# Layer 1's recombination: two 128x256 VectorE instructions out of PSUM become one 128x512 sum, and GpSimd makes the rank-1 term

## The chip, the cores and the metric

The kernel runs on one core of a Trainium2 chip. The metric is the time of one execution on the device, in microseconds (us); a run gives the median of several executions.

Five engines work side by side, each through its own fixed row of instructions: TensorE (PE in the profile, with its weight loads as PEld), VectorE (DVE), ScalarE (ACT), GpSimd (POOL) and SyncE (SP), which issues the DMA transfers. They meet through semaphores. An instruction that waits holds up everything behind it on its engine.

## The reference, cut to what matters

A two-dimensional FFT of `x` (2 x 3008 x 256, the real part is kept) gives 6016 tokens of 256 numbers. Two dense layers follow:

```python
h = x @ w_in;   g = np.maximum(h, 0) ** 2;            x1 = g @ w_out        # layer 1, d_ff = 2048
h = x1 @ w_in2; P = a0 + a1*h + a2*h**2 + a3*h**3
Q = 1 + |b0|*|h| + |b1|*h**2;  out = (P / (Q + 1e-6)) @ w_out2              # layer 2, d_ff = 2048
```

## The kernel before, in words

**Number format.** Every matrix product is made of fp32r passes: an operand is split into a high and a low part (`hi`, `lo`), and three of the four cross products are added up in PSUM.

**Tiling.** The tokens lie along the free dimension: tile 0 has 384 columns, tiles 1 to 11 have 512. `d_ff` is cut into 16 blocks of 128, so layer 1 has 16 groups per tile, written (t, j). Layer 2 works on half tiles of 256 columns and takes two blocks of `d_ff` at a time, 8 groups per half tile, with operands of 128x512 again.

**Layer 1, tiles 3 to 11.** Mirrored frequencies are used: a tile of 512 columns holds 256 columns and their 256 mirror images. The PE makes only two half products of 128x256 in one bank of PSUM (line 771): p, from the part that is even under mirroring, and b, from the odd part. The first 256 columns of h are p + b. The other 256 are p + x0*beta - b, where x0*beta is a rank-1 term (a row of tokens, held on all partitions in `X0[t]`, times a column of weights `beta[:, i]`). Tiles 0 to 2 (`DIRECT`) make both halves on the PE and skip this recombination. In each of the 9 x 16 = 144 groups of tiles 3 to 11:

- `e1_b` (ACT, L805) copies b out of PSUM into `bc` (3 buffers);
- `e1_s`, part 0 (DVE, L814) adds p out of PSUM and b into the left half of `g` (2 buffers);
- `e1_s`, part 1 (DVE, L817) makes x0*beta + p out of PSUM into the right half. It is the last reader of the PSUM bank, so it frees it;
- `e1_s`, part 2 (POOL, L820) subtracts b from the right half;
- `e1_relu` (ACT, L829), then two squares: `e1_gh` (ACT, L835, the high part of g) and `e1_g` (ACT, L839, the full g);
- `e1_lo` (POOL, L844; DVE for tiles 0 and 1) makes the low part;
- six PE matmuls of 512 columns (L796 into o1a, o1b) add the group to the tile's output.

**Layer 2.** The PE makes h (L741), and then about a dozen elementwise instructions of 128x512 follow, six of them on DVE: t2 (L881), t3 (L885), q (L873), gh (L907), m (L913) and e (L920). gh reads two operands out of SBUF; the others take h out of its PSUM bank as one operand, which e frees. c2 (POOL, L924) makes the low part, and the PE adds the group to the output (L796 into o2a). In the last two half tiles gh moves to POOL (L905) and two rows change form (L918, L898). ACT makes the copies, absolute values, reciprocal roots and squares (L862, L867, L877, L890, L894).

**Banks.** From tile 3 on, h of layer 1, h of layer 2 and the FFT pieces take turns in five PSUM banks (p0 to p3 and o2b). A row on the PE that needs a bank waits for whoever reads it last.

**Order.** All instructions belong to named operations with an engine, needs and buffers; `ORDER` is a table that fixes each engine's row of operations. The program is issued from it, and the engines then run freely under semaphores. Layer 2 of tile t needs the whole layer 1 of tile t, so layer 2 runs about one tile behind. Behind the last tile's layer 1 stand two half tiles of layer 2 that have only themselves.

**Start.** In the first 150 us the FFT's first stage, the unpacking of both layers' weights (DVE and ACT) and the direct tiles overlap.

Of the kernel before, what the change touches and what calls it, by code (L numbers as in the profile page):

```python
# [30 lines left out]
SLOTS = dict(xt=4, x1h=2, x1l=2, x0=2, x2h=2, x2l=2, ut=1, v=2, g=2, bc=3, g1=2, u=4, t1=5, y=5, g2=3, os=1,  # L31
# [18 lines left out]
def f32(ap):  # L50
# [11 lines left out]
    "05040I0J0608070K090L0A020C0M0B0N0300010O0P0Q0E0R0S0T0D0G0U0H0F0V0W0X0Y0o0Z0a1H0b0c0d0e0f0y0g0h0p0i0j"  # L62
    "0k0q0l0z0m0n1011121314150r170s160t18191B0u1A1D0v1C1F0w1E0x1G",
    ACT=
    "02030F060I0405070G0H0J0L090K080O0N0M0A0B0R0Q0P0D0C0U1Z00011a0T0S1c1i1b0X0V0W1d1f0a1e1X1g1j1Y0Y0Z2R2S"
    "0d2T1h1k2U0c2X0b2V2Y2W2Z0e0g0f2a0j2b2d2g2c2e0h0i2j2f2m0m0k2h0l2i0E0p2p2s2k0n0o2n2l2o0s0q0r2v2y2q0v2r"
    "31342t0t0u372u0y2w0w2x0x2z303A110z321033351312363D3G15383J3914173B163M3C3P193E3F183S3H3I1B1A3K3V1D3L"
    "1C3N3Y3O3b1F1l3Q1E3T3R3e1H3U3h1G1m3k1J3W3Z3X1I3a1n1L3n3q3c1o1K3f3d3g1N1M3t3w1p1P3i3j3l1O3m1q1R3o3p3r"
    "1QE33s3z1T3u1S3vEFEG1VEK423x3yEPELEQ40EH41E4431U45EIEJ44EUEVEMENERESEOETEW1WEZEaEXEY4647EeEfEbEcEdEj"
    "Ek1rEgEhEiEoEpElEmEtEuEnEq48Er49Es4A4BEvEw4CEy1sEzEx4E4D4FF3F4F84GF9F0F1F2F5F6F7FDFEFA4H4IFB4JFC4K4L"  # L70
    "FF1t4MFIFJFGFH4NFK4QFLFNFOFMFSFPFTFQ4OFR4PFYFZFU4TFVFWFdFeFaFbFcFi4RFj4S4U4VFfFXFgFkFhFl4WFn4XFmFoFs"
    "FtFxFyFp4Z4YFqG2FrFuG3FzFv4c4aG01uFw4bG7G4G1GEG5G6G84dGF4fGJ4eG9GKGA4gGB4i4hGGGHGOGI4lGLGP4jGM4k4mGT"
    "4pGN4nGU4oE54qGQGR4r4t4sGYGZGSGC4u4x4vGVGDGd4wGeGWGX1vGa4yGb4zGc50GiGjGfGg51Gh1wGn52Go5354Gk55GlGmGu"
    "59GpGqGrGv5657585A5D5B5C5HGzGwH0GxGyH45EH5H15FH25L5G5IH35J5KH6H9GsHAH75PGtHEH85M1x5NHBHF5O5T5QHC5RHD"
    "HJ5SHGHKHHHIHOHP5U5V5X5WHLHM1yHNHTHUHQ5bHR5YHSHa5ZHb5a5cHfHg5dHV5f5eHWHcHdHXHe5g5h5j5iHkHhHlHi5kHpHq"
    "5lHjHm5n1zHnHYHZ5mHoHr5o5pHu5r5qHvHzI0E6Hs5vHt5s5t5uI4I5HwHxHy5z5wI1I25x5y20I36061I9IA62I663I7I867IB"
    "ICIDIG64IH656668IL69IM6B6AIIIJ6F6CIK216DIQIR6EINIE6GIO6JIPIV6HIFIW6IIS6K22IT6NIU6L6MIXIY6RIZIaIb6O6P"
    "6QIfIg6SIcId6VIeIkIlIh6T6UIiIpIj6W6Z6XIqIm6YInIoIw6d6aIx6bJ1J26e6cIrJ6IsJ7It6fIy6gIzJ3J0J4J56hJ8J9JB"
    "JC6iIu6lIvJA6j6kJGJHJDJEJLJM6m6pJF6n23JI6oJJJK6qJQ6tJR6r6sJNJOE76uJP6x6v6wJV71JWJS6yJT6zJUJc70JXJYJd"
    "JZ24727375Jh7974JiJe76Jf77JgJmJnJj78Jk7D7AJa7BJlJbJr7CJs7HJo7EJp7FJq7GJwJxJt257IJu7JJvK17L7P7KK2JyJz"  # L80
    "K07M7N7OK6K37TK7K47QK57RKBKC7S26K8K9KA7UKIKJKD7V7XKNKOKEKFKKKLKS7WKMKT7Y7ZKX7aKPKYKQ7bKRKUKVKGKHKW7c"
    "7d7fKZ7eKcKaKdKb7j7g7hKhKi7iKe7kKf7lKg7m7nKj7rKmKnKk7o7p7qKrKl7v7sKoKs7tKp7u7zE87wKq277x7yKt83Ku87Kv"
    "8081Ky82Kz84L38B85L486L0L8L1L9L2888F89L58A8CL6KwKxL78D8ELDLELA8GLB8JLC8H8NLILJ8I8K8LLF8MLGLHLKLLLM8R"
    "LNLO8O8PLS8S8QLT8TLX8U8VLPLYLQLR8W8ZLU8X8YLVLW8dLZ29La8aLbLe8b8cLf288eLjLk8f2ALg8gLh8hLiLlLmLn8lLo8i"
    "LpLt8jLu8m8k8nLcLd8oLyLq8p8tLzLrLsLv8qLwLx8r8sM3M4M08u8v8x8wE9M1M2M5M8M9M62BM78y8z90MD912CMEMAMB92MC"
    "MK93ML9495MFMGMHMPMQMMMNMO96MUMV979899MRMSMI9DMJMTMZ9AMa9BMW9CMX9EMe9HMYMf9F9GMb9IMc9LMd9JMgMjMk9K2D"
    "Mh9M9PMi9NMl9OMoMp9Q9TMm9RMnMt9SMuMqMrMs9U2E9V9W9XN0N1Mv9bMw9YMxN59ZN6NA9aN2NBN39f9cN4N79dN89g9e9hN9"
    "9i9jNCNFNGNDMy9kMzNENK9n9l9mNL9rNHNI9oNJ9p9qNPNQNMNN9v9sNUNO9tNV9uNR9wNSNZNa9zNT9x9yA3NWEAA0NXA1NYA2"
    "NgNbNhA7NcNdA4NlNmA5Ni2FA6NqA8ABNrNjNnA9NkAANoNpNvNsNwAFACADNtAEO0Ne2GNfAJAGNuAHO1AINxAKNyANNzO5O6O2"
    "ALO3AOAMOAARAPO7O4OBAQOFOGAVASO8ATO9OCAUOMODAWOEAXAZAY2HOHONOIOJAdAaAbORAcOSOOOPAeAhAfOQAg2IOWAiOXOT"  # L90
    "AlOUAjApAkOVAmAnAoObAtOYOcOZOaAqOKArOLOgOhOdOeOfAuOlAsAvAwOmOqOiOrAxOjOnOkB1OoOpAyEBOvOwAzB0B2OsB3Ot"
    "B4B5OuB9OxOyP2P3OzB6P7B7BAB8P8BDP4P5PCBBP62JPDP9PABCBEPBBFP0PEBHP1PHBGPFPIBIPMBJPGBLBKPJPNPKBPPLBMBN"
    "2KBOPRPSBTPOBQPPPQBRBSPWPXPbPTPUPcBXBUPVBVBWBbBYPYPZPaBZBaBfPiPjPdBcPeBdPfBe2LBgBjBhPkPnPoPlBiPmBkBn"
    "BlPpPsPqPtBm2MBoPrBpBrPgBqPuPxPyBsPvBvPwBtQ2Q3PzPhBzBuQ0BwQ7Q1BxQ4ByQ8QCQ5QDQ6C3C0C1Q9ECC2C4C5QHQIC7"
    "2NC6QEQAQBQFQGC8QOQJCBQPC9CAQKQLQTQUQYCCCFCDCE2OQZQVQQCJQRCGQSCHQWCKQXCLCIQdQeQMCMCNQaQiQbQNQjQcQfQg"
    "QhQnCOCPCRCQQkQlCVQoQmCSCTCUQsCWCZCXCYQtQpQxQyQqCdQrQuCa2PCbQvCcCeQwQzChR4CfR5ClCgCiCjCkR0R12QR9CpRA"
    "CmCnR6R7R8RERFRBRCCoCqCrCtRDR2RJCsR3RKRGCuRHCxCvCwRLRMD1RICyCzRND0D2ROD3D5D4D9RPDDEDD6RTD7RUD8RQRRDA"
    "RSDBRYRZDCRVDHRWDERXDFRdReDGRaDLRbDIRcDJDPRkRlDKRfDMRgDNRhRpRmRqDORnDQDTRoDRRuRvRrDSRsDURtDXDVRzS0DW"
    "S4RwDYRxDbRyS5DZRiDaS9S1RjDcDfS2DdSAS3DeDgS6DhS7SEDjDiSFS8SBSCDkSDDnDlDmSJSKSQSGSRSHSVSISWDrSLSMDoDp"
    "SNDqSSSTSUDsDvSXSaSbSYDwSZSfDtDuSgScSkSlSODzSPSdSeDxShDySpSqSiSmSjE0SnE1SoE2SuSvSzSrSsT0EESwSxSyStT6"  # L100
    "T1T7T2TCTDTITJTOT3TPT8TUTBT9TVTaTETATFTbTGTTTHTNTKTgThTQTLTRT4TMT5TmTSTnTuTWTZTcTXTvTfTYTdTlTeU0TiU1"
    "ToTjU6TkTpU7TqTrUCUDTwU5TzTxU2TyUBU8UIU3UJU4U9UHUAUETsUFUOUGUPTtUUUKUVULUNUMUQUaUTURUfUSUZUbUWUXUYUg"
    "UcUdUeUhUiUjUkUl",
    PE=
    "0005010206040307080B090A0C0E0D0F0G0J0H0I0K0Q0S0R0L0W0M0T0N0U0O0V0X0P1C1E1G1I1D1K1M1F1H1O1Q1S1J1U1W1L"
    "1N1Y1a1P1c1R1e1T1g1V1i1X1Z1k1m1b1o1d1q1s1f1u1h1w1j1l1y201n0Y1p0Z22241r1t26281v0a1x2A2C0b1z2123252E27"
    "2G7O7Q297S2B2D2I7U2F7W7P2H7Y7a7R2J0c7T7c7V7e7X2K7Z2M7g2O0d2L7i7k7b7d7m2N2P2Q7f2S7h0e7o2U2W7q7j2Y7s2R"
    "7l7u7n7p7w7y7r2T2V7t802a2X2Z82847v2c862e7x7z0f88818A2b2g8C832d2i8E852k2f8G2m2h2j878I2o2l892q8K2n0g8B"
    "8D8M8F2s2p0h8O8H2r2u8Q2w8J8L2y302t8S8U322v2x8N8W8P8Y342z0i8R36318a8T8c3833350j8V8e3A378g8X8i8Z3C398b"
    "8k3E3B8d8m3G3D0k8f8o8h3I8q3F3K8s8j8l3H3M3J0l8n8u3O3Q3L8p8w8r8y3S3N0m8t3U3P908v923W3R3Y3T0n8x943a3V3c"  # L110
    "963e8z983X3Z9A91939C3g3b9E9G953d3i3f97993h9I9B3k9K9M9D3m9F0o3j9O3o3q3l9H9J9Q3s3n9L9S3p0p9N9U3u3w3r9P"
    "9W3y3t9R9Y403v9T9a3x0q9c42443z9V9e46419X9g430r9Z9i9k48459b9m9d9o9f4A479h4C499q9j9l4E9s4B9u9n4G4I4D9p"
    "9w4K4M4F4H9r4O0s9t4Q4J9yA04S4LA29v4U4N4P9xA4A64W4R4Y4TA89zA14a4V4XAAACA34c4e4ZA5A74g4b0uAEAG0tA94d4i"
    "0vAIAB4k4fAKAD4hAM4m4o4jAFAOAH4q4l4n0wAQAJ4pAS4s0xALANAUAW4u4rAPAYAR4w4y4tATAaAVAc4v50524xAeAX4z0yAZ"
    "5456Ag51AiAb530zAdAk585A55AmAoAf5C575E59AhAqAjAs5G5B5I5DAlAu5K5FAwAnApAy5M5H5O5JArAtB05Q5LB2Av10B45S"
    "5NAxB6Az5U5PB85W115R5Y5TBAB1BC5a5VB3B5BE5c5XBGB75Z5e12B95g5bBIBB5i5d13BK5k5f5m5hBDBM5o5jBFBOBQBH5lBS"
    "BJ5q5s5n5pBUBLBN5u5wBP5rBWBY5y5tBRBa5v14BTBcBV605xBeBX62645zBZ15Bg6661BbBiBk63686A65BdBfBm6C6716Bh6E"
    "69BoBq6G6B6I6D17BjBlBs6K6FBu6M6HBwBnByBp6O6J6LC0Br6Q18BtC2Bv6S6N6PC4C66U6R19Bx6W6TBzC8C1CA6Y6VCCC36X"
    "6aC56cC7CE6e6ZCG6b6g1AC9CBCI6i6d6k6f1BCDCK6m6hCM6o6jCFCHCOCQ6q6l6s6nCJCL6p6u6w6y6rCSCUCN6t706vCPCW6x"
    "72CY74CR6zCa7671CTCc7873CeCVCg7A75CXCi7C77CZ79Ck7ECb7BCd7GCmCoCqCf7I7DChCsCj7K7FClCuCw7MCn7H7JCyD0Cp"  # L120
    "CrD27L7NCtCvD4D6D8DADCCxDECzD1DGD3DIDKD5D7DMD9DODBDQDSDDDFDHDUDJDWDYDaDLDNDPDRDTDVDXDZDb",
    DVE=
    "0N0O000P0V0106020W030Q0X070R0Y040S080Z0T0U050a0b090d0e0c0f0A0g0C0h0B0l0i0m0D0n0j0o0k0p0E0q0F0t0G0r0H"
    "0s0u0I0K0J0L0v110w120x130y143k0z10151619171A183l1B1C1H1D1I3m1E3n1F1G1J1K1P1L481Q1M1R1S1N1T3j1U1O494A"
    "1V1X1W1Y1Z1f1a1g1b1h1c1i1d4B1j1e1k4C1n1l1o1m1p0M1q4D1v1r1w1s1x1t1y1u1z4E2023242125224F262B274G2C282D"
    "292E2A2F4H2G2J2K2H2L4I2M2I2N4J2O2R2S2P2T2Q2U4K2W2V2X4L2Y2b2Z2c2d2a2e2g4M2h2f2i4N2l2j2m2n4O2k2o4P2q2p"
    "2r2s2t4Q2v2u2w4R2x2y30312z324S33354T34363o37383A4U393B4V3C3F3D3G3H3E3I4X4W3K3J3L3M3p3N3P4Y3Q3O4Z3R3U"
# [132 lines left out]
def body(ctx: ExitStack, tc: tile.TileContext, x0, xf, w1i, w1o, w2i, w2o, a_in, b_in,  # L260
# [421 lines left out]
    for t in range(T):  # L682
# [5 lines left out]
        for i, k in enumerate(jobs):  # L688
# [18 lines left out]
            if t in DIRECT:  # L707
                add(("fn",) + key, "ACT", 0.8, lambda k=key, i=i: f_neg(*k, i), needs=[("ff",) + key],
                    take=() if k else ("y",))
# [97 lines left out]
    def e1_s(t, j, part):  # L807
        e = E1[t, j]
        n = EN[t]
        if part == 0:  # L810
            e["g"] = sb(tag2("g", t, j), [128, NMAX])[:, :e["n"]]
# [337 lines left out]
```

## Time and profile before

| what | value |
|---|---|
| median of 3 runs | 1030.74 us (1030.59 to 1030.88) |
| the profiled execution's own time | 1031.32 us |
| its span in the profile | 1029.5 us |
| granted TensorE clock | 1.0 of full speed throughout (2.4 GHz) |
| busy share of the span: PE, PEld, DVE, ACT, POOL | 98%, 93%, 96%, 92%, 59% |
| HBM traffic over the span | 36 GB/s mean; nearly all in the first 150 us |

All times of the trace come from the profiled execution: 1029.5 us of span and 1.8 us around it. It is 0.58 us over the median of the runs. A difference worked out in the trace is taken off the median.

PE, DVE and ACT are all above 90% busy, so the share of the span alone doesn't tell which one the end hangs on. One has to go stage by stage and ask who waits for whom. A matmul's end is modelled in the profile, so a matmul's duration is not what the next one costs; the distance between starts is.

### The profile page before, as it was taken

The numbers are of one execution on the slowest core, as the hardware profiler recorded it, in microseconds if no ns is written. First come the engines' busy times: TensorE is split into PE (matmuls) and PEld (weight loads), VectorE is DVE, ScalarE is ACT, GpSimd is POOL, SyncE is SP. The second block draws the span as 40 slices with busy tenths as digits, with TensorE's granted clock in tenths as the row PEclk, the third lists the DMA queues.
The fourth block names the chain that finished last, engine by engine and source line by source line (L and its number), as shares of the span: only waits on it lengthen the run. The fifth ranks groups of instructions, "written<-read, shape, count | busy, mean of one in ns | idle before, by whom it ended". The sixth has DMA issues, their size and how long they took to land.

```text
span 1029.5 us, 20583 instructions
## 1 busy us (share of the span) xinstructions
PE 1009.6 (98%) x7478; PEld 958.4 (93%) x7478; DVE 988.9 (96%) x1759; ACT 950.8 (92%) x1911; POOL 603.3 (59%) x514
## 2 busy tenths in 40 slices
PE   9999989999999999999999999999999999999996
PEld 9999979999999999999999999999998999999986
DVE  5999998899999999999999999999999999999998
ACT  3788998889899999999999999999999999999996
POOL 0000034547666776667776667677777677776486
PEclk9999999999999999999999999999999999999999
DMA  9844500000000000000000000000001000000000
GB/s 348 277 146 139 164 1 1 10 19 12 1 22 11 12 16 12 11 17 17 11 1 22 11 17 12 1 18 21 2 11 31 3 12 11 1 11 12 1 12 21
DMA packets 28256, 37.99 MB, mean 37 GB/s; under 512 B 2571, under 2 KB 20763, under 8 KB 28155
## 3 DMA queue, kind: packets, MB, share of 16 engines
q1 hardware_dynamic: 28043, 36.29, 10.4%
q8 instruction: 59, 0.97, 0.4%
q10 hardware_dynamic: 112, 0.39, 0.1%
q14 instruction: 42, 0.34, 0.1%
HBM read 27.86 MB, written 8.81 MB: 36 GB/s over the span
## 4 chain that ended last, share of the span: by engine, by line
PE 74%; ACT 10%; DVE 10%; DMA 2%; issue 2%; POOL 1%; SPq 0%; POOLq 0%; DVEq 0%; ACTq 0%
PE o2a L796 18%; PE p L741 16%; PE o1a L796 10%; PE o1b L796 10%; PE p L771 7%; PE o2b L741 4%; PE p L754 2%; PE p L756 2%; DVE g L907 1%; DMA g<-in_dram 1%; PE o2b L771 1%; ACT y L894 1%; PE o2b L796 1%; ACT y L890 1%; ACT t L867 1%
## 5 line engine op out<-in xcount | busy, mean ns | idle before, releaser
L844 POOL TENSOR_TENSOR g<-g,g 128x512 fp32r<-128x512 f32 x160 | 211.8, 1324 | 239.0 <-ACT g L839 179.1
L924 POOL TENSOR_TENSOR g<-t,y 128x512 fp32r<-128x512 f32 (+1 forms) x186 | 252.8, 1364 | 72.1 <-DVE t L920 49.4
L796 PE MATMUL o2a<-g,w2hi 128*128 128x256 f32 (+1 forms) x1440 | 255.8, 281 | 2.7 <-POOL g L924 2.6
L796 PEld LDWEIGHTS o2a<-g,w2hi 128*128 128x128 f32 x1440 | 207.2, 188 | 7.8 <-POOL g L924 3.9
L820 POOL TENSOR_TENSOR g<-g,bc 128x256 f32<-128x256 f32 x144 | 121.4, 843 | 100.6 <-DVE g L817 62.7
L796 PE MATMUL o2a<-g,w2lo 128*128 128x256 f32 (+1 forms) x720 | 143.7, 279 | 0.0
L907 DVE SCALAR_TENSOR_TENSOR g<-t,ab,y 128x512 fp32r<-128x512 f32 (+1 forms) x177 | 137.7, 779 | 4.6 <-issue 1.7
L796 PE MATMUL o1a<-g,w1hi 128*128 128x512 f32 x352 | 138.5, 393 | 0.3 <-DVE g L844 0.2
L796 PE MATMUL o1b<-g,w1hi 128*128 128x512 f32 x352 | 138.3, 393 | 0.0
L741 PE MATMUL p<-x2h,w2hi 128*128 128x256 f32 (+1 forms) x580 | 117.4, 284 | 4.8 <-ACT g L826 1.9
L894 ACT ACTIVATE y<-y 128x512 f32<-128x512 f32 (+2 forms) x187 | 119.4, 640 | 1.7
L741 PE MATMUL p<-x2h,w2lo 128*128 128x256 f32 (+1 forms) x580 | 115.9, 281 | 0.0
L741 PE MATMUL p<-x2l,w2hi 128*128 128x256 f32 (+1 forms) x580 | 115.8, 281 | 0.0
L835 ACT ACTIVATE g<-g 128x512 fp32r<-128x512 f32 (+1 forms) x170 | 108.7, 639 | 2.9 <-PE o1b L796 1.1
L885 DVE SCALAR_TENSOR_TENSOR t<-t,ab,p 128x512 f32<-128x512 f32 (+1 forms) x150 | 109.0, 727 | 1.4
L839 ACT ACTIVATE g<-g 128x512 f32<-128x512 f32 (+1 forms) x170 | 108.6, 639 | 1.5
L796 PEld LDWEIGHTS o2a<-g,w2lo 128*128 128x128 f32 x720 | 109.8, 188 | 0.0
L873 DVE SCALAR_TENSOR_TENSOR p<-u,ab,p 128x512 f32<-128x512 f32 (+1 forms) x148 | 108.4, 734 | 0.0
L920 DVE SCALAR_TENSOR_TENSOR t<-t,ab,p 128x512 f32<-128x512 f32 (+1 forms) x144 | 104.5, 727 | 1.3
L913 DVE SCALAR_TENSOR_TENSOR p<-p,g 128x512 f32<-128x512 f32 (+1 forms) x153 | 103.6, 678 | 1.3
L867 ACT ACTIVATE t<-p,ab 128x512 f32<-128x512 f32 (+1 forms) x150 | 103.2, 689 | 0.4 <-POOL g L924 0.4
L881 DVE TENSOR_TENSOR t<-t,p 128x512 f32<-128x512 f32 (+1 forms) x150 | 99.7, 666 | 3.5 <-ACT t L867 2.7
(255 smaller groups left out, 2739.3 us busy)
## 6 DMA issues: line engine op xcount, KB each, us to landing
g<-in_dram SPq DMA_DIRECT2D x48, 256.0 KB
xt<-in_dram SPq DMA_DIRECT2D x15, 384.0 KB
out_dram<-os SPq DMA_DIRECT2D x22, 256.0 KB
udram<-U SPq DMA_DIRECT2D x4, 640.0 KB
ut<-udram SPq DMA_DIRECT2D x10, 256.0 KB
x2h<-in_dram SPq DMA_DIRECT2D x8, 256.0 KB
x2l<-in_dram SPq DMA_DIRECT2D x8, 256.0 KB
x<-qdram SPq DMA_DIRECT2D x9, 128.0 KB
```

The lines of the kernel that those rows point to most:

```text
L741: nc.tensor.matmul(h[:, c * n:(c + 1) * n], l[:, k, :], r[:, k], start=(q == 0), stop=(q == 5))
L796: nc.tensor.matmul(O[t][e], l[:, e * 128:(e + 1) * 128], r[:, c * n:(c + 1) * n], start=(i == 0 and q == 0 and (e == 0 or not one)), stop= ...
L820: nc.gpsimd.tensor_tensor(out=g[:, 1], in0=g[:, 1], in1=b, op=ALU.subtract)
L835: nc.scalar.activation(out=e["gh"], in_=e["g"], func=ACTF.Square)
L839: nc.scalar.activation(out=e["g"], in_=e["g"], func=ACTF.Square)
L844: eng.tensor_tensor(out=e["gl"], in0=e["g"], in1=f32(e["gh"]), op=ALU.subtract)
L867: nc.scalar.activation(out=e["t1"], in_=H2[t, j], func=ACTF.Identity, scale=SCALES[0], bias=a2)
L873: nc.vector.scalar_tensor_tensor(out=e["w"], in0=w, scalar=b0, in1=H2[t, j], op0=ALU.add, op1=ALU.mult)
L885: nc.vector.scalar_tensor_tensor(out=e["t1"], in0=e["t1"], scalar=a1, in1=H2[t, j], op0=ALU.add, op1=ALU.mult)
L894: nc.scalar.activation(out=z, in_=z, func=ACTF.Square)
L907: nc.vector.scalar_tensor_tensor(out=e["gh"], in0=e["t1"], scalar=a0, in1=e["z"], op0=ALU.add, op1=ALU.mult)
L924: (nc.vector if (t, j) in FIN else nc.gpsimd).tensor_tensor(out=e["gl"], in0=e["t1"], in1=e["z"], op=ALU.mult)
```

## The change

Per group of tiles 3 to 11 the two DVE instructions and the POOL subtraction become one DVE instruction and two on POOL, in another order:

- ACT copies b straight into the left half of `g` (L807). `bc` is gone; `g` has 3 buffers in place of 2, and there is one new buffer `xb` (128x256). The SBUF in use is the same: 7 KB per partition.
- POOL makes `xb` = x0*beta (`e1_x`, L812), which needs nothing of the PE's, and then `xb` - b into the right half of `g` (`e1_n`, L816).
- DVE adds p, read out of PSUM twice over (a broadcast along the halves), onto all 512 columns of `g` in place (`e1_s`, L820). It now frees the PSUM bank, and the ReLU waits for DVE, no more for POOL.
- A negation in the direct tiles (`fn`) is held in order behind its first part.
- `ORDER` is a new table for all five engines.

```diff
-SLOTS = dict(xt=4, x1h=2, x1l=2, x0=2, x2h=2, x2l=2, ut=1, v=2, g=2, bc=3, g1=2, u=4, t1=5, y=5, g2=3, os=1,
+SLOTS = dict(xt=4, x1h=2, x1l=2, x0=2, x2h=2, x2l=2, ut=1, v=2, g=3, xb=1, g1=2, u=4, t1=5, y=5, g2=3, os=1,
...
     SP=
-    "05040I0J0608070K090L0A020C0M0B0N0300010O0P0Q0E0R0S0T0D0G0U0H0F0V0W0X0Y0o0Z0a1H0b0c0d0e0f0y0g0h0p0i0j"
+    "05040I060J0208070K090L0A030M0C0B0N00010O0P0Q0R0G0S0o0T0U0H0V0W0E0X0F0Y0Z0a0D1H0y0b0c0d0e0f0g0h0i0j0k"
...
                 add(("fn",) + key, "ACT", 0.8, lambda k=key, i=i: f_neg(*k, i), needs=[("ff",) + key],
-                    take=() if k else ("y",))
+                    take=() if k else ("y",), after=[("fn", t, 0)] if k else [])
...
-        e["b"] = sb("bc", [128, NMAX // 2])[:, :gs * n].rearrange("p (c n) -> p c n", c=gs)
-        nc.scalar.activation(out=e["b"], in_=H1[t, j][:, 1], func=ACTF.Copy)
...
-            nc.vector.tensor_tensor(out=g[:, 0], in0=H1[t, j][:, 0, 0], in1=b, op=ALU.add)
...
-            nc.vector.scalar_tensor_tensor(out=g[:, 1], in0=X0[t], scalar=beta[:, i:i + 1], in1=H1.pop((t, j))[:, 0, 0],
-                                           op0=ALU.mult, op1=ALU.add)
-        else:
-            nc.gpsimd.tensor_tensor(out=g[:, 1], in0=g[:, 1], in1=b, op=ALU.subtract)
+        e["g"] = sb(tag2("g", t, j), [128, NMAX])[:, :e["n"]]
+        e["s"] = e["g"].rearrange("p (s n) -> p s n", s=2)
+        nc.scalar.activation(out=e["s"][:, 0], in_=H1[t, j][:, 1, 0], func=ACTF.Copy)
+
+    def e1_x(t, j):
+        i = GROUPS1[t][j][0]
+        XB[t, j] = sb("xb", [128, NMAX // 2])
+        nc.gpsimd.tensor_scalar(out=XB[t, j], in0=X0[t], scalar1=beta[:, i:i + 1], scalar2=None, op0=ALU.mult)
+
+    def e1_n(t, j):
+        g = E1[t, j]["s"]
+        nc.gpsimd.tensor_tensor(out=g[:, 1], in0=XB.pop((t, j)), in1=g[:, 0], op=ALU.subtract)
+
+    def e1_s(t, j):
+        g = E1[t, j]["s"]
+        nc.vector.tensor_tensor(out=g, in0=H1.pop((t, j))[:, 0].to_broadcast([128, 2, EN[t]]), in1=g, op=ALU.add)
```

What the new table does is seen in the rows of the engines. A name with a number is a buffer of one group; p_10101, o2b and the like are PSUM banks, x_75 is `X0[t]`. First DVE in the middle of the program, at layer 1's groups (9, 6) and (9, 7), before:

```order
L907 SCALAR_TENSOR_TENSOR g_10119<-t_9986,ab,y 128x512
L814 TENSOR_TENSOR g<-p_10101,bc 128x256
L913 SCALAR_TENSOR_TENSOR o2b<-o2b,g_10119 128x512
L817 SCALAR_TENSOR_TENSOR g<-x_75,beta,p_10101 128x256
L920 SCALAR_TENSOR_TENSOR t_9986<-t_9986,ab,o2b 128x512
L881 TENSOR_TENSOR t_10133<-t_10133,p_10059 128x512
L814 TENSOR_TENSOR g<-p_10110,bc 128x256
L817 SCALAR_TENSOR_TENSOR g<-x_75,beta,p_10110 128x256
```

and the same place of DVE in the changed program:

```order
L820 TENSOR_TENSOR g<-o2b,g 128x512
L913 SCALAR_TENSOR_TENSOR p_9934<-p_9934,g_10110 128x512
L873 SCALAR_TENSOR_TENSOR p_10061<-u,ab,p_10061 128x512
L920 SCALAR_TENSOR_TENSOR t_9981<-t_9981,ab,p_9934 128x512
L907 SCALAR_TENSOR_TENSOR g_10185<-t_10059,ab,y 128x512
L820 TENSOR_TENSOR g<-p_10093,g 128x512
L913 SCALAR_TENSOR_TENSOR p_10011<-p_10011,g_10185 128x512
```

The pair L814, L817 has become one row, L820, between the rows of layer 2. POOL at the same groups, before:

```order
L820 TENSOR_TENSOR g<-g,bc 128x256
L924 TENSOR_TENSOR g_10119<-t_9986,y 128x512
L844 TENSOR_TENSOR g_10177<-g,g_10177 128x512
L820 TENSOR_TENSOR g<-g,bc 128x256
L844 TENSOR_TENSOR g_10245<-g,g_10245 128x512
```

and in the changed program:

```order
L812 TENSOR_SCALAR xb<-x_75,beta 128x256
L844 TENSOR_TENSOR g_10026<-g,g_10026 128x512
L924 TENSOR_TENSOR g_9985<-t_9879,y 128x512
L924 TENSOR_TENSOR g_10028<-t_9930,y 128x512
L816 TENSOR_TENSOR g<-xb,g 128x256
L812 TENSOR_SCALAR xb<-x_75,beta 128x256
L844 TENSOR_TENSOR g_10117<-g,g_10117 128x512
L816 TENSOR_TENSOR g<-xb,g 128x256
```

L816 has taken the place of the old L820, and a row L812 has come in ahead of each; with one buffer `xb`, an L812 always stands behind the L816 before it. The PE's row keeps its shape: in both programs 170 of layer 2's 193 groups are finished when layer 1's last group is, and 23 follow.

## Rows read from the trace of the kernel before

**Rows 1.** The page: busy us, share of the span, instructions, by engine.

```profile
PE 1009.6 (98%) x7478; PEld 958.4 (93%) x7478; DVE 988.9 (96%) x1759; ACT 950.8 (92%) x1911; POOL 603.3 (59%) x514
```

**Rows 2.** Busy us by stage; first column the stretch and its length.

```profile
0.00:150.00 150.00, 143.89 (x1004) 136.13 (x1005) 134.94 (x312) 117.55 (x263) 6.71 (x10) 1.00 0.54 185
150.00:235.00 85.00, 84.98 (x591) 81.88 (x590) 77.62 (x130) 72.42 (x147) 40.35 (x34) 1.00 0.03 9
235.00:950.00 715.00, 712.95 (x5353) 676.26 (x5353) 701.90 (x1196) 691.09 (x1370) 504.65 (x434) 1.00 0.04 12
950.00:1000.00 50.00, 47.00 (x374) 44.95 (x373) 50.00 (x81) 48.35 (x92) 30.88 (x24) 1.00 0.04 12
1000.00:1029.50 29.50, 20.77 (x164) 19.19 (x162) 24.43 (x45) 21.38 (x44) 20.76 (x16) 1.00 0.05 18
```

**Rows 3.** Timeline of PE: start us, duration us, line, out<-in, count [idle before <-releaser].

```profile
314.06 0.39 PE L796 MATMUL o1a<-g,w1hi 128*128 128x512 f32 x1
314.29 0.39 PE L796 MATMUL o1b<-g,w1hi 128*128 128x512 f32 x1
314.52 0.40 PE L796 MATMUL o2a<-g,w2hi 128*128 128x256 f32 x2
314.75 0.40 PE L796 MATMUL o2a<-g,w2lo 128*128 128x256 f32 x2
```

**Rows 4.** Waits of PE, 235 to 950 us (us in total, times, longest us).

```profile
PE p L741 <- DVE g L817: 0.8, 1, 0.8
PE o2b L741 <- DVE g L817: 0.7, 1, 0.7
PE p L771 <- DVE g L817: 0.4, 1, 0.4
```

**Rows 5.** Waits of PE, first 150 us, the two longest of six.

```profile
PE p L741 <- ACT g L826: 1.9, 1, 1.9
PE p L741 <- DVE t L920: 1.2, 1, 1.2
```

**Rows 6.** Waits of PE, 950 us to the end, the longest two of five.

```profile
PE o2a L796 <- POOL g L924: 2.6, 4, 1.1
PE o1b L741 <- DVE t L918: 2.5, 2, 2.1
```

**Rows 7.** Groups on DVE by form: xcount | busy us, mean ns | idle before.

```profile
L907 DVE SCALAR_TENSOR_TENSOR g<-t,ab,y 128x512 fp32r<-128x512 f32 x160 | 126.6, 792 | 4.0 <-issue 1.5 <-ACT y L894 1.0 <-PE o2a L796 0.2
L885 DVE SCALAR_TENSOR_TENSOR t<-t,ab,p 128x512 f32<-128x512 f32 x134 | 99.3, 742 | 1.2
L881 DVE TENSOR_TENSOR t<-t,p 128x512 f32<-128x512 f32 x134 | 91.0, 680 | 2.0 <-ACT t L867 1.4
L817 DVE SCALAR_TENSOR_TENSOR g<-x,beta,p 128x256 f32<-128x256 f32 x118 | 55.7, 472 | 0.0
L814 DVE TENSOR_TENSOR g<-p,bc 128x256 f32<-128x256 f32 x118 | 49.3, 418 | 3.8 <-POOL g L844 1.7 <-ACT bc L805 1.3 <-POOL g L820 0.4
```

**Rows 8.** Groups on POOL and two on ACT, by form.

```profile
L924 POOL TENSOR_TENSOR g<-t,y 128x512 fp32r<-128x512 f32 x170 | 235.6, 1390 | 49.6 <-DVE t L920 35.5 <-ACT g L826 2.6 <-ACT g L835 2.3
L844 POOL TENSOR_TENSOR g<-g,g 128x512 fp32r<-128x512 f32 x160 | 211.8, 1324 | 239.0 <-ACT g L839 179.1 <-issue 40.2 <-POOL g L924 9.5
L820 POOL TENSOR_TENSOR g<-g,bc 128x256 f32<-128x256 f32 x144 | 121.4, 843 | 100.6 <-DVE g L817 62.7 <-ACT t L867 5.8 <-ACT g L839 5.6
L829 ACT ACTIVATE g<-g 128x512 f32<-128x512 f32 x144 | 92.5, 642 | 6.4 <-POOL g L820 5.8
L805 ACT ACTIVATE bc<-p 128x256 f32<-128x256 f32 x118 | 46.3, 393 | 0.8 <-PE p L771 0.6
```

**Rows 9.** Timeline around the longest wait of rows 4.

```profile
791.83 2.61 POOL L924 TENSOR_TENSOR g<-t,y 128x512 fp32r<-128x512 f32 x2
...
793.05 1.93 DVE L907 SCALAR_TENSOR_TENSOR g<-t,ab,y 128x512 fp32r<-128x512 f32 x1
...
794.91 0.41 DVE L814 TENSOR_TENSOR g<-p,bc 128x256 f32<-128x256 f32 x1
...
795.24 0.47 DVE L817 SCALAR_TENSOR_TENSOR g<-x,beta,p 128x256 f32<-128x256 f32 x1
...
795.85 0.47 PE L741 MATMUL p<-x2h,w2hi 128*128 128x256 f32 x2 [0.80 <-DVE g L817]
```

## What the change should do to the time

> **What bounds the kernel now.** I read four views, in this order. The page's first part shows three engines close together, PE 98%, DVE 96%, ACT 92% [rows 1]; that is an average and decides nothing. The stretches by stage [rows 2] split it. In the first 150 us PE lacks 6.1 us of being busy throughout (150 - 143.89) while weights are unpacked. From 150 to 950 us it lacks 0.02 + 2.05 us. From 950 us on it lacks 3.0 + 8.7 us, while DVE shows 50.00 busy out of 50 between 950 and 1000 us. So there are two regimes: to 950 us PE sets the pace, behind it DVE does, with ACT (48.35 of 50) next to it.
>
> A busy PE row is not yet a full PE, since matmul ends are modelled. The timeline settles it [rows 3]: a 512-column matmul, though shown as 0.39 us long, has the next one 0.23 us behind its start, and a pair of 256-column ones takes the same 0.23 us. Starts stand this close without a gap over nearly the whole middle, at a granted clock of 1.0 [rows 2]. 715 us of middle hold 5353 matmuls; nothing in the change takes one of them away.
>
> The third view is who PE waits for. In the 715 us of the middle there are three waits, 1.9 us in all, and all three are for L817 on DVE, the instruction that the change removes [rows 4]. The fourth view, the timeline around the longest of them [rows 9], shows how it comes about: a gh (L907) takes 1.93 us in place of its mean of 0.792 [rows 7] while POOL runs two L924; L814 and L817 stand behind it on DVE; L817 frees a PSUM bank late, and PE stands 0.80 us.
>
> **The change, part by part.** *DVE.* Removed: 144 x (0.418 + 0.472) us [rows 7]; the count of groups is that of L820 [rows 8]. Added: 144 sums of 128x512 with one operand in PSUM and one in SBUF. The trace before has just this form in L881: 0.680 us [rows 7]. Its first operand is read twice over, which no row shows; the far bound is 0.792, the longest mean of a 128x512 row on DVE [rows 7]. I take 0.680, the same operation from the same two memories. Saved: 144 x 0.210 = 30.2 us of DVE time (14.1 us by the far bound). How much of that reaches the end? In the middle DVE is not what PE lacks: only 2.05 us of PE idle time stand there, 1.9 us of it named. That is the most the middle can give: **1.9 us**, not 30.
>
> *POOL.* Added: 144 products of 128x256 with one tensor operand (L812). No such row exists. Bounds: 0.843 us, the 128x256 subtraction with two tensor operands [rows 8], and from below 0.36 us, the part of POOL's time that does not grow with columns: the 256 columns that L844 has over L820 cost 1.324 - 0.843 = 0.48, which leaves 0.843 - 0.48 [rows 8]. With one operand to read in place of two I estimate it midway, at 0.60 us. That is 86 us more (52 to 121). In the middle POOL is busy 504.65 of 715 us [rows 2], so it rises from 71% to 83% (78% to 88%). It still isn't full. The subtraction itself (old L820, new L816) keeps its size, but it waits now for ACT's copy instead of L817 on DVE: of its 100.6 us of idle time 62.7 were spent on L817 [rows 8], and the copy ends earlier than L817 did. What is queued behind a waiting L816 is L844 and L924, on which o1 and o2 of the PE wait.
>
> *The chain of one group.* Before, from PE's half products to ReLU: 0.393 + 0.418 + 0.472 + 0.843 = 2.13 us without waits. Now 0.393 + 0.843 + 0.680 = 1.92 us, with one change of engine at the same number of places (ACT, POOL, DVE, ACT in place of ACT, DVE, POOL, ACT). ACT does the same four instructions; its ReLU waited 5.8 us in all for POOL [rows 8] and now waits for DVE. None of this is on PE's path while PE has other groups to go on with. The group's bank, however, used to be free after 0.393 + 0.418 + 0.472 = 1.28 us and now after 1.92, POOL's queue between: 0.63 us longer at least. That is a cost, and I come back to it as a rival. The third `g` buffer pays for b's copy standing in it longer; at 0 us, covered by the third buffer; without it ACT's copy would wait for an L844.
>
> *The end.* DVE has no idle time from 950 to 1000 us, so the time is DVE's rows behind layer 1's last group, and they are layer 2's alone. PE's row has 23 groups left there in both programs, and DVE's has the same six operations for them; the change takes nothing out. DVE might arrive less late, since it has had slack until then; ACT leaves room for 50 - 48.35 = 1.65 us of that [rows 2]. I take half of it: **0.8 us** (0 to 1.65).
>
> *The start.* The tables of SP, ACT and DVE are new there as well, with the same instructions. The waits that a bank's turn could remove or double are 1.9 and 1.2 us [rows 5]. I take 0 (3.1 us either way); SP issues the same transfers, and the middle moves little on it.
>
> *Sum.* 1.9 + 0.8 + 0 = 2.7 us off the span of 1029.5 us, and as much off the median: 1030.74 - 2.7 = **1028.0 us**. (The profiled execution stood at 1031.32, 0.58 us over the median, so differences alone are carried over.)
>
> **A page of the Trainium skill against this reading.** By starts in rows 3, PE has no room in the middle. The Trainium skill, Perfetto Trace Analysis, section Identifying the Most-Contended Engine, says that matmul busy time is a poor measure, and that the share of weight loads should be used. That share is 676.26 of 715, 94.6% [rows 2]. By that measure PE would have 38.7 us of room in the middle, more than the 30.2 us that DVE gives back, and the sum would be rival D's. The trace doesn't bear it out: starts 0.23 us apart without a gap [rows 3] mean a PE that is full at 94.6% of weight loads.
>
> **The rivals.**
> *A, the forecast: faster by 2.7 us,* 1028.0; own range 1025.5 to 1030.
> *B, the waits come back elsewhere: no change,* 1030.5. For it: POOL at 83% will run beside gh more often, and the wait of rows 9 began with a gh of 1.93 us beside POOL. The Trainium skill, SBUF — State Buffer, section Who interferes with whom, has this as a rule: a VectorE instruction with two SBUF inputs and a GpSimd one that reads SBUF block each other for a whole instruction. The trace agrees in the 1.93 us. By rows the price is small: gh's mean exceeds that of L885 by 0.05 us [rows 7], 8 us over 160 rows; at 83/71 of that, 1.4 us more for a DVE that has 30 us less to do.
> *C, slower: the bank comes free through POOL's queue.* The hold of 1.92 us grows by up to a whole L924 of 1.39 us [rows 8] whenever POOL has just begun one. PE then stands where a bank is due, as in rows 9, at 0.7 us a time (the middle one of rows 4). It decides from four such waits on, where 1.9 + 0.8 us are spent. With one wait per tile of the nine: 9 x 0.7 = 6.3 us, which gives 1030.74 - 2.7 + 6.3 = 1034.3; with two in some tiles, 1036. Against it: five banks take turns, and PE's row is nearly the old one.
> *D, DVE sets the pace everywhere,* as its 96% suggests: all 30.2 us come back, 1000.5. Against it: rows 3 and 4.
> *E, start and end gain as well.* The two long waits of the start, 3.1 us [rows 5], vanish, and of the two long ones of the end, 5.1 us [rows 6], a third: 1028.0 - 3.1 - 1.7 = 1023.2.
>
> **How the numbers follow.** A measurement of this kernel can tell about 0.2%, 2.06 us, from no change: faster is below 1028.7, slower above 1032.8. Chances: A 0.45, B 0.20, C 0.18, E 0.12, D 0.05. Of A's own range about three quarters lies below 1028.7 (0.33). Faster: 0.33 + 0.12 + 0.05 = 0.50; same: 0.12 + 0.20 = 0.32; slower: 0.18. The range takes in A, B, E with the start's bound on its far side, and C up to one wait per tile: 1022 to 1035. It leaves out D and the worse half of C and a little of E.
>
> **What would show it.** In the profile of the changed kernel: L820 on DVE at 0.68 us x144 and DVE's busy time down by about 30 us, to some 959 (its share near 93%); if it reads above 0.79, the broadcast costs. L812 near 0.60 us and POOL's share near 67% of the span. The starts of PE's matmuls still 0.23 us apart, and its busy time in the middle not below 712 of 715. No wait for L817; if waits of PE on DVE L820 add up to over 4 us, C has happened. The last L796 into o1a about 2 us earlier than the layer's end before, and the stretch behind it as long as before, within 1 us. The prediction is wrong in kind if the middle shrinks by more than 3 us, which PE's starts forbid, or if the first 150 us move by more than 3.1.

## The result and the profile after

The changed kernel took **1043.91 us** (median of 4 runs, 1042.5 to 1045.79) where the kernel before took 1030.66: ratio 1.013, interval 1.0111 to 1.015. It is 13.3 us slower. The forecast was 2.7 us faster, with a range up to 1035; both missed. The profiled execution of after took 1042.5 us, with a span of 1040.3.

The page's first part and two of the stretches (length, then the busy time of each engine with its instructions, the granted clock, DMA share, GB/s):

```profile
PE 1017.1 (98%) x7478; PEld 960.0 (92%) x7478; DVE 992.9 (95%) x1615; ACT 953.1 (92%) x1911; POOL 733.1 (70%) x658
...
0.00:150.00 150.00, 143.33 (x1006) 135.91 (x1007) 135.13 (x313) 118.87 (x263) 7.69 (x10) 1.00 0.54 184
...
235.00:950.00 715.00, 710.17 (x5266) 667.58 (x5266) 695.28 (x1034) 680.78 (x1349) 625.82 (x568) 1.00 0.04 12
```

Set this beside [rows 1, 2]. The start is unchanged (143.33 us of PE against 143.89). The middle is not: 87 matmuls fewer lie in the same 715 us (5266 against 5353). DVE has 144 instructions fewer and yet 4 us *more* busy time than before. POOL rose from 504.65 to 625.82 us of the middle, 87.5%. The last matmul into layer 1's output starts at 972.7 us where it stood at 960.6, and what follows it is about as long as before (67.6 and 68.9 us). So the whole loss is made in the middle. (The two profiled executions differ by 10.8 us of span, less than the medians: the profiled one of after was its fastest.)

Which rows of DVE grew? Groups by line and form (busy us, mean ns, then idle time before them), then the row of the view of one line that has min/median/max, first after and then before:

```profile
L907 DVE SCALAR_TENSOR_TENSOR g<-t,ab,y 128x512 fp32r<-128x512 f32 x160 | 145.0, 907 | 5.7 <-ACT y L894 3.2 <-issue 0.7 <-PE o2a L796 0.5
...
L881 DVE TENSOR_TENSOR t<-t,p 128x512 f32<-128x512 f32 x128 | 86.7, 678 | 1.4 <-POOL g L844 0.5 <-ACT t L867 0.5
L820 DVE TENSOR_TENSOR g<-p,g 128x512 f32<-128x512 f32 x123 | 84.0, 683 | 6.1 <-POOL g L816 5.3
```
```profile
L907 DVE SCALAR_TENSOR_TENSOR g<-t,ab,y x176: 606/751/1872, 140.3 to 985.1; 128x512 fp32r<-128x512 f32 x160, 128x384 fp32r<-128x384 f32 x16
```
```profile
L907 DVE SCALAR_TENSOR_TENSOR g<-t,ab,y x177: 543/747/1934, 140.7 to 1022.6; 128x512 fp32r<-128x512 f32 x160, 128x384 fp32r<-128x384 f32 x16, 128x256 fp32r<-128x256 f32 x1
```

Only gh (L907) grew: its mean went from 792 [rows 7] to 907 ns while the median stayed (747, 751). So it isn't slower throughout; some of its instructions are far longer. Counted over the 160 of 128x512: 10 lasted above 0.9 us before, 53 after; what stands above 0.747 us adds up to 7.5 us before and **26.0** after. I call them long gh below.

The new rows of POOL, of one line and by groups:

```profile
L812 POOL TENSOR_SCALAR xb<-x,beta x144: 913/926/1437, 223.5 to 952.1; 128x256 f32<-128x256 f32 x144
```
```profile
L924 POOL TENSOR_TENSOR g<-t,y 128x512 fp32r<-128x512 f32 x167 | 227.4, 1365 | 34.0 <-DVE t L920 28.0 <-PE o1b L796 3.4 <-PE p L771 0.9
...
L812 POOL TENSOR_SCALAR xb<-x,beta 128x256 f32<-128x256 f32 x144 | 142.5, 989 | 4.7
L816 POOL TENSOR_TENSOR g<-xb,g 128x256 f32<-128x256 f32 x144 | 115.8, 804 | 43.3 <-ACT g L807 36.4 <-DVE p L913 1.4 <-DVE g L907 1.3
```

Who PE waits for between 150 and 975 us, all rows (us, times, longest):

```profile
PE p L741 <- DVE g L820: 2.1, 6, 0.8
PE o2b L741 <- DVE g L820: 1.3, 3, 0.7
PE p L741 <- DVE t L920: 0.8, 2, 0.5
PE p L771 <- DVE g L820: 0.4, 2, 0.2
PE p L771 <- DVE t L920: 0.2, 1, 0.2
```

Against three waits in [rows 4]: fourteen, 4.8 us, all for a bank that DVE frees. That view shows only part of it. By the distance between the starts of neighbouring matmuls, less 0.229 us for 512 columns and 0.113 for 256 or fewer, PE stood 10.4 us in all between 240 and 945 us before, and 22.0 after. I use this sum, "PE lost", from here on. Only its differences between kernels are to be relied on: a base longer or shorter by 1 ns would move every entry alike by some 5 us. The timeline at one wait shows how it comes about:

```profile
925.97 1.87 DVE L907 SCALAR_TENSOR_TENSOR g<-t,ab,y 128x512 fp32r<-128x512 f32 x1
925.97 1.32 POOL L924 TENSOR_TENSOR g<-t,y 128x512 fp32r<-128x512 f32 x1
...
927.27 1.35 POOL L812 TENSOR_SCALAR xb<-x,beta 128x256 f32<-128x256 f32 x1
...
927.76 0.68 DVE L820 TENSOR_TENSOR g<-p,g 128x512 f32<-128x512 f32 x1
928.36 0.68 DVE L913 SCALAR_TENSOR_TENSOR o2b<-o2b,g 128x512 f32<-128x512 f32 x1
928.47 0.64 ACT L829 ACTIVATE g<-g 128x512 f32<-128x512 f32 x1 [0.29 <-DVE g L820]
...
928.58 0.47 PE L741 MATMUL p<-x2h,w2hi 128*128 128x256 f32 x2 [0.75 <-DVE g L820]
```

It is the picture of [rows 9] with L820 in L817's place: a gh and an L924 start together, gh takes 1.87 us for 0.75, the sum behind it frees a bank 1.1 us late, and PE stands 0.75 us.

### The profile page after: what moved, and what is told of

It reads as the page before. It is cut to its first block, busy times and chain, and to the rows that moved or that the text cites. A ratio compares the mean times of both kernels' runs of the same rounds, so it can differ in the third digit from the quotient of the medians.

```text
span 1040.3 us, 20487 instructions
## 1 busy us (share of the span) xinstructions
PE 1017.1 (98%) x7478; PEld 960.0 (92%) x7478; DVE 992.9 (95%) x1615; ACT 953.1 (92%) x1911; POOL 733.1 (70%) x658
## 3 DMA queue, kind: packets, MB, share of 16 engines
q1 hardware_dynamic: 28043, 36.29, 10.4%
## 4 chain that ended last, share of the span: by engine, by line
PE 58%; DVE 17%; ACT 16%; issue 4%; POOL 3%; DMA 1%; SPq 0%; POOLq 0%; ACTq 0%; DVEq 0%
PE o2a L796 14%; PE p L741 12%; PE o1a L796 7%; PE o1b L796 7%; PE p L771 5%; DVE g L907 3%; PE o2b L741 3%; PE p L756 3%; PE p L754 3%; DVE g L820 2%; DVE t L881 2%; DVE p L913 2%; ACT t L867 2%; DVE p L873 2%; DVE t L885 2%
## 5 line engine op out<-in xcount | busy, mean ns | idle before, releaser
L844 POOL TENSOR_TENSOR g<-g,g 128x512 fp32r<-128x512 f32 x160 | 213.8, 1338 | 187.2 <-ACT g L839 179.5
L924 POOL TENSOR_TENSOR g<-t,y 128x512 fp32r<-128x512 f32 (+1 forms) x183 | 244.3, 1338 | 57.8 <-DVE t L920 43.5
L907 DVE SCALAR_TENSOR_TENSOR g<-t,ab,y 128x512 fp32r<-128x512 f32 (+1 forms) x176 | 154.8, 881 | 8.4 <-ACT y L894 5.2
L816 POOL TENSOR_TENSOR g<-xb,g 128x256 f32<-128x256 f32 x144 | 115.8, 804 | 43.3 <-ACT g L807 36.4
L812 POOL TENSOR_SCALAR xb<-x,beta 128x256 f32<-128x256 f32 x144 | 142.5, 989 | 4.7
L894 ACT ACTIVATE y<-y 128x512 f32<-128x512 f32 (+1 forms) x186 | 116.4, 627 | 1.7
L741 PE MATMUL p<-x2h,w2lo 128*128 128x256 f32 (+1 forms) x566 | 113.3, 282 | 0.0
L741 PE MATMUL p<-x2l,w2hi 128*128 128x256 f32 (+1 forms) x566 | 113.0, 281 | 0.0
L885 DVE SCALAR_TENSOR_TENSOR t<-t,ab,p 128x512 f32<-128x512 f32 (+1 forms) x144 | 104.3, 725 | 1.5
L829 ACT ACTIVATE g<-g 128x512 f32<-128x512 f32 x144 | 91.3, 634 | 14.0 <-DVE g L820 13.0
L920 DVE SCALAR_TENSOR_TENSOR t<-t,ab,p 128x512 f32<-128x512 f32 (+1 forms) x140 | 101.5, 725 | 1.7
L913 DVE SCALAR_TENSOR_TENSOR p<-p,g 128x512 f32<-128x512 f32 (+1 forms) x150 | 101.0, 675 | 1.8
```

Source lines behind the costliest of these rows:

```text
L741: nc.tensor.matmul(h[:, c * n:(c + 1) * n], l[:, k, :], r[:, k], start=(q == 0), stop=(q == 5))
L812: nc.gpsimd.tensor_scalar(out=XB[t, j], in0=X0[t], scalar1=beta[:, i:i + 1], scalar2=None, op0=ALU.mult)
L816: nc.gpsimd.tensor_tensor(out=g[:, 1], in0=XB.pop((t, j)), in1=g[:, 0], op=ALU.subtract)
L844: eng.tensor_tensor(out=e["gl"], in0=e["g"], in1=f32(e["gh"]), op=ALU.subtract)
L885: nc.vector.scalar_tensor_tensor(out=e["t1"], in0=e["t1"], scalar=a1, in1=H2[t, j], op0=ALU.add, op1=ALU.mult)
L894: nc.scalar.activation(out=z, in_=z, func=ACTF.Square)
```

## Experiments

The theories, with the letters that the later expectations use (those of e1, e2, e4 and e7, the first four to run, have letters of their own, told in them, and so have single later ones). **C**, collisions: gh takes two operands from SBUF, a GpSimd instruction that reads SBUF at the same time holds it up, and a fuller GpSimd row meets gh more often. **L**: the product's length (0.99 us, estimated at 0.60) makes this worse. Rivals: GpSimd is late and delays PE without any collision; **T**, the new table, or **R**, the table or the longer chain, does it; **W**, gh's wait for z. "Before" in a ratio is the kernel before, run beside that variant (medians of 1030.7 to 1031.3 us).

| kernel | us | ratio to before, interval | long gh of 160, excess us | PE lost, 240 to 945 us |
|---|---|---|---|---|
| before | 1030.7 | 1 | 10, 7.5 | 10.4 |
| after | 1043.9 | 1.0130, 1.0111 to 1.0150 | 53, 26.0 | 22.0 |
| e7: after, gh with one SBUF operand, no wait for z | 1029.7 | 0.9985, 0.9971 to 1.0000 | 0, 0 | 9.2 |
| e9: the same, wait for z kept | 1031.1 | 1.0011, 0.9987 to 1.0036 | 0, 0 | 10.7 |
| e7b: before, gh as in e7 | 1026.4 | 0.9959, 0.9946 to 0.9971 | 0, 0 | 6.1 |
| e17: before, gh as in e9 | 1027.5 | 0.9963, 0.9951 to 0.9976 | 0, 0 | 6.3 |
| e1: after without the product | 1038.6 | 1.0069, 1.0048 to 1.0091 | 22, 16.2 | 15.5 |
| e5: after, product of two operands | 1033.8 | 1.0038, 1.0023 to 1.0053 | 34, 17.0 | 13.7 |
| e16: after, product by a constant | 1039.7 | 1.0094, 1.0071 to 1.0118 | 50, 22.9 | 19.0 |
| e12: e5 and e9 | 1029.3 | 0.9986, 0.9976 to 0.9996 | 0, 0 | 10.0 |
| e13: e1 and e9 | 1029.1 | 0.9978, 0.9964 to 0.9993 | 0, 0 | 9.1 |
| e4: after, the sum in two halves | 1047.8 | 1.0160, 1.0126 to 1.0195 | 50, 23.4 | 26.8 |
| e2: before with a product | 1075.6 | 1.0425, 1.0390 to 1.0459 | 39, 19.1 | 52.3 |
| e11: after in before's table | 1088.3 | 1.0560, 1.0542 to 1.0577 | 64, 36.1 | 59.6 |
| e15: e11 and e9 | 1059.5 | 1.0274, 1.0257 to 1.0292 | 0, 0 | 38.0 |

### Is it the collisions? e7, e9, e7b, e17

```diff
 # e7 (in after), e7b (in before)
-  nc.vector.scalar_tensor_tensor(out=e["gh"], in0=e["t1"], scalar=a0, in1=e["z"], ...)
+  nc.vector.scalar_tensor_tensor(out=e["gh"], in0=e["t1"], scalar=a0, in1=H2[t, j], ...)
 # e9 (in after), e17 (in before)
+  nc.vector.scalar_tensor_tensor(out=e["gh"], in0=e["t1"], scalar=e["z"][:, 0:1], in1=H2[t, j], ...)
```

> The changed kernel with gh (L907) reading its second operand out of the PSUM bank (w) instead of z out of SBUF, so that it has one SBUF operand; gh then has another value (the reciprocal is left out of it) and no longer waits for z. Same engines, same table, GpSimd as full as in the changed kernel. Theory P by way of the collisions between gh and GpSimd: L907 falls from 0.907 to about 0.75 us mean, VectorE gets 18 to 25 us back, time 1030 to 1038 us. Theory P by way of GpSimd's lateness alone, and theories C and T: 1041 to 1045 us.

> The changed kernel with gh reading w out of PSUM as its second operand, as in e7, but with the first column of z as its scalar operand (so the product is not the reference's): it waits for z as ever, and reads one full operand of SBUF in place of two. Theory C (collisions with GpSimd's reads): as e7, 1028 to 1032, no gh above 0.9 us, mean 0.74. Theory W (e7's gain was the dropped wait for z): nothing comes back, 1040 to 1045. Between them: 1033 to 1038.

> The kernel before with one edit: gh takes w out of PSUM as its second operand in place of z out of SBUF (so the value of the low part is not the reference's). Theory C (a gh with two SBUF operands is held up by GpSimd): gh's 10 long ones of 160 vanish, mean 0.74 us in place of 0.792; PE has only 2 us of idle time in the middle to give back, and the end behind 950 us, where DVE has no idle time, gives about 23 x 0.05 = 1 us: 1027 to 1030, faster by 1 to 4 us. Theory W (the changed kernel gained 14 us by this edit because gh no longer waits for z, not because of collisions): the same edit should help before by a like amount, wherever z ends last, and the end by more: 1018 to 1025.

> The kernel before with gh on one SBUF operand as in e9: w from PSUM, the first column of z as its scalar, so that it waits for z as ever (its product is not the reference's). e7b, which also dropped the wait for z, took 1026.4; the changed kernel without collisions took 1031.1 with its product and 1029.3 with the shorter one. Theory W' (the wait for z is what e7b gained beyond these): 1028 to 1029.5, as much as e12 and e13, so that nothing of the change's loss is left without collisions but the product's length. Theory R' (the new rows or the chain through GpSimd cost some 2 to 3 us by themselves): 1026 to 1027.5, as e7b.

e9's gh, its page, its middle, and all of its PE's waits of the middle:

```profile
L907 DVE SCALAR_TENSOR_TENSOR g<-t,y,p x140: 600/741/750, 140.8 to 966.4; 128x512 fp32r<-128x512 f32 x124, 128x384 fp32r<-128x384 f32 x16
```
```profile
PE 1010.7 (98%) x7478; PEld 959.5 (93%) x7478; DVE 969.1 (94%) x1615; ACT 951.2 (92%) x1911; POOL 701.5 (68%) x658
```
```profile
235.00:950.00 715.00, 714.43 (x5352) 677.44 (x5351) 683.90 (x1053) 690.55 (x1371) 603.26 (x575) 1.00 0.04 12
```
```profile
PE p L741 <- DVE t L920: 0.3, 1, 0.3
PE p L741 <- DVE g L820: 0.2, 1, 0.2
```

The longest gh is 0.750 us, and 12.8 us of the 13.3 come back, although POOL is still 84% busy in the middle, with 603.26 of 715 us. So a GpSimd that full costs PE little by its lateness, as long as it does not hold gh up. W falls too: e9 keeps the wait for z and gains nearly what e7 does. The same edit takes 3.8 us (0.37%) out of before (e17), where I had seen 2 us of idle time to be had. So the collisions that the change added are worth 12.3 - 3.8 = 8.5 us (by the ratios of the table), not all that e9 gives back. e7b's 1026.4 lay between what C (1027 to 1030) and W (1018 to 1025) had said of it. e17 came out at the edge of R' (1026 to 1027.5), not at W' (1028 to 1029.5): even without collisions the changed kernel keeps a loss of its own over before.

The long gh don't stand beside all of POOL's rows alike. At the start of gh in after, POOL was idle 39 times (99 before), in L924 41 times (25 of these gh long), in L844 28 times (17), in L816 19 times (9), in L812 33 times (2). The Trainium skill, SBUF — State Buffer, section Who interferes with whom, says that a DVE instruction with two SBUF inputs contends with a GpSimd instruction that reads SBUF. e9 agrees, with 53 long gh against 0 by the number of SBUF operands alone; the 2 of 33 beside L812, which reads SBUF as well, are fewer than that rule suggests.

### The product's length and form: e5, e16, e1, e12, e13

```diff
 # e5, e12
-  nc.gpsimd.tensor_scalar(out=XB[t, j], in0=X0[t], scalar1=beta[:, i:i + 1], scalar2=None, op0=ALU.mult)
+  nc.gpsimd.tensor_tensor(out=XB[t, j], in0=X0[t], in1=beta[:, i:i + 1].to_broadcast([128, NMAX // 2]), op=ALU.mult)
 # e16
+  nc.gpsimd.tensor_scalar(out=XB[t, j], in0=X0[t], scalar1=0.5, scalar2=None, op0=ALU.mult)
 # e1, e13
+  XB[t, j] = X0[t]
```

> The changed kernel without the 144 products L812 on GpSimd: L816 subtracts from X0[t] itself, so the scaling of the rank-1 term by beta is left out. Nothing else moves, the table of sequences stays. Theory P (GpSimd is too full: L812 takes 0.93 to 0.99 us in place of the 0.60 that was estimated, so POOL is 87.5% busy in the middle, the low parts and the subtraction come later, and gh on VectorE meets a reading GpSimd more often): POOL falls to some 70% in the middle, L907 to under 0.82 us mean, time 1024 to 1032 us. Theory C (the bank of layer 1 comes free late because its release now passes through GpSimd's queue at all): the chain is unchanged, time stays at 1038 or above. Theory T (the new table is worse by itself): 1040 or above.

> The changed kernel with GpSimd's product written as an operation of two tensor operands, the second a column of beta broadcast along the row; the values are the same. The subtraction in that form has a median of 0.75 us, the product now 0.93. Theory L (the product's length makes GpSimd late, so that more of its reading rows meet a gh): product 0.75 us, GpSimd's busy time down by 144 x 0.18 = 26 us, gh's long ones fall from 53 to about 35, 1036 to 1041. Theory C in its narrow form (a product of one tensor operand does not hold gh up, one of two does, since 2 of 33 products beside a gh did): each product saved in length becomes a new collision, gh's long ones stay at 50 to 80, 1041 to 1048.

> The changed kernel with a constant, 0.5, in place of the column of beta as the product's scalar operand (so the rank-1 term is not the reference's). Theory V (it is the scalar read from SBUF that makes GpSimd's product 0.93 us): 0.5 to 0.7 us, GpSimd's busy time down by 35 to 60 us, long gh at 25 to 40, 1032 to 1038. Theory F (the operation with one tensor operand is as slow with a constant): 0.9 us or more, 1041 to 1046 like the changed kernel.

> e5 and e9 together: the changed kernel with the product as an operation of two tensor operands (0.66 us) and gh with one SBUF operand (its product is not the reference's, its wait for z is kept). Theory C+L (collisions and the product's length are all that the change lost; the rest is sound): PE's idle time in the middle falls to that of before without collisions, 1026 to 1029. Theory R (the chain ACT, GpSimd, DVE ahead of the bank costs by itself, or the new table does): it stays at e9's time, 1030 to 1032.

> e1 and e9 together: the changed kernel without the 144 products (the subtraction takes x0 as it is) and gh with one SBUF operand, its wait for z kept; neither result is the reference's. GpSimd is as full as in the kernel before, and nothing holds gh up. Theory C+L: 1026 to 1030. Theory R: 1031 to 1036, since e1 still stood 7 us over before with 22 long gh, and these were not the whole of it.

The product's row (min/median/max ns) in e5, then in e16; above, in after, it read 913/926/1437:

```profile
L812 POOL TENSOR_TENSOR xb<-x,beta x144: 602/614/1127, 222.8 to 942.8; 128x256 f32<-128x256 f32 x144
```
```profile
L812 POOL TENSOR_SCALAR xb<-x x144: 839/851/1325, 222.7 to 948.2; 128x256 f32<-128x256 f32 x144
```

The same product, over the same columns, takes 0.61 us with beta as a broadcast second tensor and 0.93 as a scalar; a constant scalar saves only 0.075. So it is the form of the operation that is long (F), not the read of the scalar (V), though both of F's ranges (0.9 us or more, 1041 to 1046) were missed by a little. e5 computes what after computes, in the same rows, and gets 10.1 us of the 13.3 back: 34 long gh for 53. L holds, below its lower edge (1036): the product became shorter than the 0.75 us expected. Both columns of the table move together from after over e16 to e5: excess 26.0, 22.9, 17.0 us; 1043.9, 1039.7, 1033.8. The narrow reading of C (a short product of two operands would only make new collisions) has something in it, 7 long gh of 27 beside the new L812, but far too little.

e1 was to come to 1024 to 1032 if the product alone made the loss, and to 1038 or more otherwise; it took 1038.6. Without the product POOL's middle holds 492.15 us, less than before, and yet 22 gh are long with 16.2 us of excess, as much as in e5. The product is thus not the only thing that sets GpSimd against gh; the rows' new places are left as a reason, which no run here isolates. In e1 POOL is in an instruction at the start of 63 gh, hardly more often than before (61), where only 10 were long. Some 3.5 us of e1's time, by its profile, aren't in the middle at all but in the first 15 us. Its matmuls took nearly twice as long there as those of e13, which has the same rows; a pair at the same place, first in e1, then in e13:

```profile
11.03 0.89 PE L358 MATMUL p<-c_t,xt 128*128 128x188 f32 x2
```
```profile
8.93 0.51 PE L358 MATMUL p<-c_t,xt 128*128 128x188 f32 x2
```

From 15 us on both run alike, and e1's PE is 3.5 us later. The granted clock reads 1.00 in both; why the matmuls were slow there stays open, and so does whether e1's other executions began like this. Less that, the profiled execution of 1039.4 would stand at some 1036, nearer to e5. e13 shows that the product without collisions is cheap: 1029.1 without it, 1029.3 with the short one (e12), 1031.1 with the long one (e9). e13 speaks for C+L, while e12 lies between C+L (to 1029) and R (from 1030). R falls in the size that was expected; what is left of it are the 1.5 and 2.4 us by which e13 and e12 stand over e17.

### The table: e11, e15, e2

```diff
 # e2 (in before)
         else:
+            i = GROUPS1[t][j][0]
+            nc.gpsimd.tensor_scalar(out=sb("xb", [128, NMAX // 2]), in0=X0[t], scalar1=beta[:, i:i + 1], ...)
             nc.gpsimd.tensor_tensor(out=g[:, 1], in0=g[:, 1], in1=b, op=ALU.subtract)
 # e11: ORDER is before's; DVE's s1 (L820) at the place of before's L817, the product ahead of L816
```

> The kernel before, with its own table, plus one product of 128x256 on GpSimd per layer-1 group, issued right ahead of L820's subtraction, whose result nobody reads (one buffer of 1 KB more). Theory P: GpSimd gets 144 x 0.93 to 0.99 = 134 to 143 us more, gh is held up more often (L907 from 0.79 to about 0.9 us mean), time 1038 to 1046 us. Theories C and T: neither the chain's engines nor the table change for VectorE and TensorE, 1029 to 1033 us.

> The changed kernel's arithmetic in the rows of the kernel before: PE, ACT and SP have before's table, DVE has its one sum at the place of before's second 128x256 instruction, GpSimd has the product just ahead of the subtraction. Theory T (the new table set gh against GpSimd's reading rows; the arithmetic itself is sound): gh's long ones at 25 or fewer of 160, 1030 to 1036. Theory A (a GpSimd that is 87% full in the middle meets gh whatever the table): 45 or more long ones, 1040 to 1055; worse than the changed kernel is possible, since that table was not made for GpSimd's longer rows (before with a dead product added took 1075.6).

> e11 (the changed arithmetic in the rows of the kernel before, 1088 us) with gh on one SBUF operand, its wait for z kept; the product of gh is not the reference's. Theory C (collisions explain that kernel too, 64 long gh of 160): 1035 to 1050. Theory S (in those rows the sum stands on DVE ahead of rows that could go on and waits for GpSimd, 43 us of idle time before it): most of the loss stays, 1060 to 1082, and the idle time before the sum too.

What stood ahead of the sum L820 on DVE (us, times) in e11, and then in e15; in after this row reads 7.0, 19:

```profile
  POOL g L816: 50.2, 52
```
```profile
  POOL g L816: 52.7, 64
```

T falls, the other way round: in before's rows the same arithmetic takes 1088 us, so the new table is worth 44 us to it. A had its count right (64 long gh), its time (1040 to 1055) far too low. e15, just below S's range, splits the loss: without collisions 1059.5, still 28 us over before, and DVE stands 52.7 us at the sum, waiting for L816 on POOL. That is rival C of the prediction, real in rows that put the sum too early, and nearly absent in the new rows (e9: PE waits 0.2 us for L820).

e2 went in the expected direction and four times as far (+44.8 us for 8 to 15 expected). A dead product ahead of the subtraction, which nobody waits for, delays everything behind it on POOL in rows that were not made for it. It bears on rows that don't give way, and says little on after, whose table does.

### What DVE saves: e4

```diff
-  nc.vector.tensor_tensor(out=g, in0=H1.pop((t, j))[:, 0].to_broadcast([128, 2, EN[t]]), in1=g, op=ALU.add)
+  h = H1.pop((t, j))[:, 0, 0]
+  nc.vector.tensor_tensor(out=g[:, 0], in0=h, in1=g[:, 0], op=ALU.add)
+  nc.vector.tensor_tensor(out=g[:, 1], in0=h, in1=g[:, 1], op=ALU.add)
```

> The changed kernel with the one 128x512 sum L820 undone into two sums of 128x256 (left and right half, same operands, same place in the row). From starts to starts on VectorE a 128x512 sum holds the engine 0.60 us and two of 128x256 hold it 2 x 0.34 = 0.68 us: 144 x 0.08 = 11 us more VectorE time. If VectorE limits the middle of the changed kernel together with GpSimd (theory P): 1048 to 1056 us. If VectorE has slack there (as the prediction had it) and the loss is only the bank's longer hold (theory C): the hold grows by 0.08 us of 5.2, 1043 to 1045 us.

The two halves and, from after, the sum in one:

```profile
L821 DVE TENSOR_TENSOR g<-p,g 128x256 f32<-128x256 f32 x123 | 51.2, 416 | 5.4 <-POOL g L816 4.5
L822 DVE TENSOR_TENSOR g<-p,g 128x256 f32<-128x256 f32 x123 | 50.6, 411 | 0.0
```

By these durations two halves cost 416 + 411 - 683 = 144 ns more than the whole sum, 21 us over 144 groups; the time grew by only 3.9 (3.1 by the ratios, whose intervals overlap). Durations overlap on DVE: the median distance from start to start is 334 and 331 ns for the halves and 601 for the sum, so 64 ns more, 9 us. Of the two expectations the one of 1048 to 1056 missed by a hair and the one of 1043 to 1045 by 3 us: DVE's time seems to count in this kernel, at a third to a half; how much of it is not shown this closely.

## Why the prediction was wrong

The step that failed is the cost of POOL's extra work. The sum put it at nothing, since POOL at 83% "still isn't full", and rival B priced the longer gh beside it at 1.4 us. The runs show 18.5 us more of gh's excess, of which 8.5 us reach the time. Beside it, the price of L812 and DVE's saving were mis-sized.

**Where the 13.3 us are.** In ratios to before: collisions cost after 1.0130 - 1.0011, 12.3 us; before had them too, 1 - 0.9963, 3.8 us; without any, the change costs 1.0011 - 0.9963, 4.9 us. 12.3 - 3.8 + 4.9 = 13.4. Of the 4.9, the product's long form would be 1.0011 - 0.9986, 2.6 us, but the intervals of e9 and e12 overlap, so this share is not shown by itself. The cause of the last 2.4 (e12 over e17) stays open: their intervals just touch, and PE's losses (10.0 against 6.3 us) lie between 240 and 750 us without a wait that stands out.

Point by point:

- **L812 at 0.60 us, at most 0.843: wrong.** It measured 0.989 (0.925 undisturbed, in e9). I took one tensor operand for less work than two. The nearest row, a subtraction of two, was no upper bound for another form of operation; the 0.60 fits the form that the change didn't use (0.61, e5). POOL's 87.5% of the middle lay inside my 78 to 88% only because less of its other work fitted into the slower middle: 504.65 us and 142 products there of 0.987 would have been 645, not 625.82.
- **L820 at 0.680 us: right** (0.683), and the broadcast costs nothing.
- **DVE saves 30.2 us: mis-sized.** From start to start the old pair took 334 + 389 ns and the sum takes 601: 122 ns, 17.6 us. [rows 9] had it: L814 lasts 0.41 us and L817 starts 0.33 behind it. I read starts for PE and durations for DVE. Collisions then took 26.0 - 7.5 = 18.5 us, and nothing was left (988.9 to 992.9 us busy).
- **The middle can give 1.9 us: too little.** e17 took 3.8 out of before by ending its ten long gh. The waits view names waits of some length; PE's small losses behind them aren't in it: by starts e17 has 4.1 us less of them than before (6.3 for 10.4).
- **Rival B's mechanism, at a thirteenth of its size.** The price of "1.4 us more" took gh's mean excess, 0.05 us, as a rate that grows with POOL's busy share. It is not a rate but single events of 0.15 to 1.2 us (0.46 us on average in after), whose number follows how POOL's rows fall beside gh: 10, 22, 34, 39, 50, 53 and 64 in the kernels here. Doubling the places at which POOL is in an instruction when gh starts (61 to 121 of 160) made them five times as many. And I set that price against DVE's gain as if DVE had slack, when a long gh sits ahead of the row that frees PE's bank.
- **Rival C, the bank through POOL's queue: the right direction by the wrong cause,** and too small (1034.3 to 1036). Waits for L820 come to 3.8 us in the waits view, close to the 4 us from which I would have called it C. e9 shows that they were gh's doing: 0.2 us without collisions.
- **Rival D** is out by e9 as well: DVE at 94% with 24 us less to do than in after, and the time stays at PE's 1031. The Trainium skill's share of weight loads (Perfetto Trace Analysis, section Identifying the Most-Contended Engine) would read 677.44 of 715 us there, 94.7%, with a PE that e9's row shows busy for 714.43.
- **The start at 0: right** (143.33 us of PE against 143.89). **The end, 0.8 us off: inside its range** of 0 to 1.65. The stretch from layer 1's last matmul on is 1.3 us shorter in after (67.6 us for 68.9), and without collisions 1.2 us (67.5 in e9, 68.6 in e17); that DVE's slack is the reason was not tested. Rival E's 4.8 us of start and end did not come.

No version here that still computes the reference beats the kernel before; e5 is the nearest, 0.38% over it, in rows that were laid out for another length of the product.

## What to carry to other kernels

Before work is moved to an engine whose instructions can hold up those of another, count events, not means: how often an instruction of one meets an instruction of the other now, what one meeting costs, and who stands behind it. Take the price of an operation from a row of the same form, and when a gain is read off durations, check it against the distance between starts. An expensive-looking form is worth a second spelling: here the same product as an operation of two tensors gave back 10 of 13 us.

## What the runs showed of the hardware

On GpSimd a 128x256 product with one tensor operand and a scalar column took 0.926 us, with a constant 0.851, and with the column broadcast as a second tensor 0.614, less than the 0.745 of a subtraction of two full tensors (L816 in e9). A gh that meets an L924 or L844 can last longer by most of that row's length (1.87 us for 0.75 beside an L924 of 1.32). GpSimd's rows seem to be held up in their turn: L812's longest is 1.437 us in after and 0.949 in e9, where gh takes only one of its tensors from SBUF. The two rows of e9:

```profile
L812 POOL TENSOR_SCALAR xb<-x,beta x144: 913/925/949, 224.4 to 941.1; 128x256 f32<-128x256 f32 x144
```
```profile
L816 POOL TENSOR_TENSOR g<-xb,g x144: 727/745/768, 235.7 to 949.8; 128x256 f32<-128x256 f32 x144
```
